# Loading three operands of a gated linear attention kernel with two tokens in a row per partition in place of four

## The chip, the cores and the metric

The kernel runs on one core of a Trainium2 chip. The core has a matrix engine (TensorE, "PE" in the profile), a vector engine (VectorE, "DVE"), a scalar engine (ScalarE, "ACT"), GpSimd ("POOL") and SyncE ("SP"), which in this kernel issues every DMA. Each engine works through its own list of instructions in order and waits on semaphores for the others. The metric is the device time of one execution in microseconds (us); lower is better.

## The reference

The program is a gated linear attention over 768 tokens for 4 batches and 8 heads of 48 channels, followed by a feed-forward block on the 3072 tokens with 384 channels:

```python
for t in range(S):
    state = alpha[:, :, t, :, None] * state + np.einsum('bhd,bhe->bhde', k[:, :, t], v[:, :, t])
    y[:, :, t] = np.einsum('bhd,bhde->bhe', q[:, :, t], state)

x = attn_out.transpose(0, 2, 1, 3).reshape(B * S, H * D)
h = x @ w_in                       # 384 -> 2048
g = h * np.clip(h + 3.0, 0.0, 6.0) / 6.0
out = g @ w_out                    # 2048 -> 384
```

All inputs of the attention are float32.

## The kernel before

The tokens are cut into 24 chunks of 128 (`j` runs from 0 to 23, six to a batch), and chunks go in pairs (`g`) through the feed-forward block. The heads are held in four pairs (`p`, up to `NP` = 4), each pair on 128 partitions: 48 channels of one head, 16 of padding, 48 of the other, 16 of padding.

For a chunk the attention needs alpha, k and q with the channels on the partitions and the tokens along the free dimension. In DRAM a head's data lie token by token, 48 channels each. For chunks 0 to 5 they are loaded as they lie and transposed on TensorE (L282). For chunks 6 to 23 (`FIRST` is 6) this is done with the DVE's transpose of 32x32 blocks, and the DMA that loads the chunk (`load_akq`, L262) puts the data where these blocks need them. That DMA is split into four, one for each group of 32 partitions: heads of one parity and 32 channels (groups 0 and 2), or the last 16 channels (groups 1 and 3; the load begins 32 channels later, and the end of the row is set to 1.0 by the memsets at L257 the first time a buffer is used). Partition `u` of a group holds the four tokens `4u` to `4u + 3` in a row, 4 x 48 channels for each of four head pairs. So one DMA has 32 x 4 pieces of 192 or 160 floats (768 or 640 bytes). There are two buffers for each of alpha, k and q (`quads`, named `aq`, `kq` and `qq` in the profile).

`by_blocks` (L286) then transposes 4 x 4 blocks for each group of partitions in one DVE instruction. A block gives 32 tokens of one place `v` out of four, and they are written to `4u + v`: neighbours in a block lie four floats, 16 bytes, apart.

From these come, on DVE, the products of alpha backwards and forwards (two scans, L309 and L320), k and q scaled by them (L332), on PE the scores (L346), the update of the state (L429) and the output (L455). From chunk 8 on the scaled k goes token by token again without PE: `turn_k` (word `kt`, L391) transposes blocks in place of the raw k, `write_k` (`kw`, four DMAs, L396) writes them to DRAM, and `read_k` (`kr`, four DMAs, L404) reads them back as `kb`, which the state's update reads. v comes in by two DMAs a chunk (`lv`, L272), outputs leave by L728.

The feed-forward block uses sums of weight and activation blocks (L537 to L541, words `y`, `xc`, `o`) so that fewer products are needed: products into the hidden layer at L600 (word `M`), out of it at L703 (word `P`).

The order of all engines' work is one list of words at the end of the function, `run("""...""")`, read by `steps`. `la.9` loads alpha of chunk 9, `ca.9` transposes it, `lk`/`tk` and `lq`/`tq` do the same for k and q; `O.1.1` stores an output block, `y.22` makes a weight sum. Each engine takes its instructions in the order of the list; nothing is reordered. SP has one in-order queue for all DMAs. A DMA that has to wait for its buffer or for its data holds up all those behind it. A part of the list around chunk 9:

```python
M.2.10 cy.6 ck.7 sc.7.0.2 u.7.1.3 n.2.10.14 M.2.11 qa.7.1 ca.9 la.11 y.22 M.2.6.2
h.2.1 q.8 m.7 e.2.0.0 h.2.0 n.2.11.15 qa.6.0 n.2.18.10 qa.8.1 M.2.12 M.2.19
```

Each DMA signals one of eight semaphores, taken in turn, so a DMA is issued only when the eighth one before it has landed.

Of the kernel before, what the change touches and what calls it, by code (L numbers as in the profile page):

```python
# [17 lines left out]
def kernel(  # L18
# [32 lines left out]
    nc = tc.nc  # L51
    B, H, S, D = q.shape
# [35 lines left out]
    for r in range(NR):  # L88
        for name, pad in (("a", 1.0), ("k", 0.0), ("q", 0.0)):
            t = ring[name, r] = rings[:, 3 * r + "akq".index(name)]  # L90
# [3 lines left out]
    for r in range(NV):  # L94
        t = consts.tile([C, 2, H, 64], FP, tag=f"v{r}", name=f"v{r}")
        nc.gpsimd.memset(t, 0.0)
        vs.append(t)
    for r in range(2):
        t = consts.tile([C, 2, H, HB], FP, tag=f"A{r}", name=f"A{r}")
# [6 lines left out]
    for r in range(2):  # L106
        t = consts.tile([C, NP * W + 1], FP, tag=f"ax{r}")
        nc.vector.memset(t, 0.0)
        aX.append(t)
        t = consts.tile([C, NP * W], FP, tag=f"ini{r}")  # L110
# [122 lines left out]

    BLK = 32
    V = C // BLK
    FIRST = 6
    NQ = 2
    quads = {}
    for r in range(NQ):
        for name in "akq":  # L240
            quads[name, r] = consts.tile([C, NP, V, D], FP, tag=f"{name}q{r}",
                                         name=f"{name}q{r}")

    def rows(t, j):
        b, c = divmod(j, NC)
        return t[b, :, c * C : (c + 1) * C, :]

    def load_akq(name, j):
        src = rows({"a": alpha, "k": k, "q": q}[name], j)
        if j < FIRST:  # L250
            nc.sync.dma_start(out=ring[name, j % NR][:, :, 0:D],
                              in_=src.rearrange("h s d -> s h d"))
            return
        to = quads[name, j % NQ]
        if j < FIRST + NQ:
            for o in (BLK, 3 * BLK):
                nc.gpsimd.memset(to[o : o + BLK, :, V - 1, D - BLK : BLK], 1.0)  # L257
        to = to.rearrange("r p v d -> r p (v d)")
        t = src.rearrange("(p a) (u v) d -> a u p (v d)", a=2, v=V)
        for o in range(4):  # L260
            skip = BLK * (o % 2)
            nc.sync.dma_start(out=to[BLK * o : BLK * (o + 1), :, 0 : V * D - skip],  # L262
                              in_=t[o // 2, :, :, skip : V * D])

    v_t = {}

# [7 lines left out]
    def transposed(name, j, i=None):  # L274
        if j >= FIRST:
            t = (K_t if name == "k" else Q_t)[j] = (Ks if name == "k" else Qs)[j % 2]
            by_blocks(t, name, j)
            return
        t = bank("t" + name, j, i)
        src = ring[name, j % NR]  # L280
        for p in range(NP):
            nc.tensor.transpose(  # L282
                t[:, p], src[:, 2 * p : 2 * p + 2].rearrange("s h d -> s (h d)"), ident)

    def by_blocks(to, name, j):
        nc.vector.transpose(out=to.rearrange("r p (u v) -> r p v u", v=V),  # L286
                            in_=quads[name, j % NQ][:, :, :, 0:BLK])

    def reverse(t, first, n):

# [3 lines left out]
    def without_first(t):  # L294
        return t[:, 0 : NP * W].rearrange("r (p w) -> r p w", w=W)[:, :, 1:W]

    def place_alpha(j):
        to = without_first(aX[j % 2])
        if j < FIRST:
            nc.scalar.copy(out=to, in_=ps_t.pop(("ta", j)))  # L300
        else:
            by_blocks(to, "a", j)
# [21 lines left out]
    def scaled(name, j):  # L324

        if j < FIRST:
            src = ps_t.pop(("t" + name, j))
# [244 lines left out]
    for i in range(8):  # L572
        r, o = divmod(i, 3)
# [70 lines left out]
    t = {1: b[0, 1], 2: spare[:, 0], 3: spare[:, 1], 4: spare[:, 2]}  # L644
# [80 lines left out]
    def store2(g, i):  # L725
# [5 lines left out]

    steps = {
        "la": lambda j: load_akq("a", j), "lk": lambda j: load_akq("k", j),
        "lq": lambda j: load_akq("q", j), "lv": load_v, "w": load_weight,
        "d1": round_low, "d2": magnitude, "dx": sign, "d3": high_bits, "d4": add_low,
        "ta": lambda j, *i: transposed("a", j, *i), "tk": lambda j, *i: transposed("k", j, *i),
# [202 lines left out]
```

## Time and profile before

The median of three runs is 539.71 us (539.61 to 539.85). The table is of one profiled execution.

| what | value |
|---|---|
| span of the profiled execution | 538.1 us |
| PE, weight loads, DVE, ACT, POOL busy | 526.3, 499.7, 475.3, 259.6, 50.4 us |
| granted PE clock | 1.00 in all stretches |
| DMA | 54.40 MB in 124101 packets, 101 GB/s on average |
| alpha, k and q loads of chunks 6 on | 216 DMAs, 96 or 80 KB each, about 2.5 us from issue to landing |
| transposes by L286 | 54, 60.2 us in all |

"Busy" counts an engine's own instructions; the issue of a DMA does not count. In groups of instructions the two numbers behind the bar are the total busy time and the mean time of one in nanoseconds; then follows how long the engine stood idle just before them. In lists of waits the numbers are the total, how many, and the longest. In timelines the first number is the start, the second the length, both in us, of a row of equal instructions. "SPq" is the queue of SP.

### The profile page before, as it was taken

The numbers are of one execution on the slowest core, as the hardware profiler recorded it, in microseconds if no ns is written. First come the engines' busy times: TensorE is split into PE (matmuls) and PEld (weight loads), VectorE is DVE, ScalarE is ACT, GpSimd is POOL, SyncE is SP. The second block draws the span as 40 slices with busy tenths as digits, with TensorE's granted clock in tenths as the row PEclk, the third lists the DMA queues.
The fourth block names the chain that finished last, engine by engine and source line by source line (L and its number), as shares of the span: only waits on it lengthen the run. The fifth ranks groups of instructions, "written<-read, shape, count | busy, mean of one in ns | idle before, by whom it ended". The sixth has DMA issues, their size and how long they took to land.

```text
span 538.1 us, 15166 instructions
## 1 busy us (share of the span) xinstructions
PE 526.3 (98%) x6306; PEld 499.7 (93%) x6306; DVE 475.3 (88%) x839; ACT 259.6 (48%) x513; POOL 50.4 (9%) x71
## 2 busy tenths in 40 slices
PE   8799999999999999999999999999999999999997
PEld 7688886789999999999999999999999999999996
DVE  6999989999999899989999898999999898495481
ACT  3889865212653553543544444642644544553230
POOL 5333425100000000000010000000000000000000
PEclk9999999999999999999999999999999999999999
DMA  9998876006625156263444355155354042100001
GB/s 172 211 251 250 218 217 154 17 2 154 149 35 117 30 117 141 46 140 86 94 109 112 89 121 137 21 127 120 88 136 103 15 103 42 44 3 1 15 16 37
DMA packets 124101, 54.40 MB, mean 101 GB/s; under 512 B 83329, under 2 KB 116865, under 8 KB 124033
## 3 DMA queue, kind: packets, MB, share of 16 engines
q1 hardware_dynamic: 124032, 53.44, 43.7%
q8 instruction: 49, 0.80, 0.7%
q14 instruction: 20, 0.16, 0.1%
HBM read 44.50 MB, written 8.91 MB: 99 GB/s over the span
## 4 chain that ended last, share of the span: by engine, by line
PE 83%; DVE 10%; DMA 3%; ACT 1%; issue 1%; SPq 0%; POOL 0%; DVEq 0%; ACTq 0%; POOLq 0%
PE m_ps L703 32%; PE m_ps L600 32%; PE m_ps L478 6%; PE t_ps L455 4%; PE t_ps L346 2%; PE t_ps L429 2%; DMA v<-in_v_dram 2%; PE m_ps L532 1%; PE m_ps L489 1%; PE m_ps L516 1%; DVE rings L647 1%; DVE R L309 1%; DVE raw L537 1%; DVE g_sb L647 1%; DVE w L537 1%
## 5 line engine op out<-in xcount | busy, mean ns | idle before, releaser
L703 PE MATMUL m_ps<-w,g_sb 128*128 128x192 f32 x704 | 122.1, 327 | 0.6 <-ACT m_ps L709 0.5
L606 ACT COPY g_sb<-m_ps 128x512 f32<-128x512 f32 x110 | 63.5, 584 | 114.7 <-PE m_ps L600 98.2
L703 PEld LDWEIGHTS m_ps<-w,g_sb 128*128 128x128 f32 x704 | 113.7, 190 | 1.7 <-ACT m_ps L709 0.8
L703 PE MATMUL m_ps<-rings,g_sb 128*128 128x192 f32 x528 | 91.6, 327 | 0.6 <-ACT u L682 0.6
L703 PEld LDWEIGHTS m_ps<-rings,g_sb 128*128 128x128 f32 x528 | 85.3, 190 | 1.0 <-ACT u L682 0.9
L600 PE MATMUL m_ps<-xc,w 128*128 128x128 f32 x640 | 82.7, 277 | 0.2 <-DVE w L541 0.2
L600 PEld LDWEIGHTS m_ps<-xc,w 128*128 128x128 f32 x640 | 77.5, 192 | 1.4 <-issue 0.4
L494 ACT ACTIVATE r<-g_sb,half 128x512 f32<-128x512 f32 x80 | 56.7, 722 | 29.4 <-DVE g_sb L541 11.7
L498 DVE SCALAR_TENSOR_TENSOR g_sb<-r,g_sb 128x512 f32<-128x512 f32 x80 | 53.6, 682 | 7.5 <-ACT r L494 7.0
L600 PE MATMUL m_ps<-xT,raw 128*128 128x128 f32 x400 | 52.6, 278 | 0.9 <-ACT g_sb L606 0.9
L600 PEld LDWEIGHTS m_ps<-xT,raw 128*128 128x128 f32 x400 | 48.6, 192 | 1.9 <-ACT g_sb L606 1.2
L409 POOL TENSOR_TENSOR st<-sm,R 128x192 f32<-128x192 f32 x20 | 12.9, 643 | 355.8 <-DVE sm L439 306.7
L647 DVE TENSOR_TENSOR g_sb<-g_sb 128x512 f32<-128x512 f32 (+1 forms) x55 | 42.0, 792 | 1.4 <-PE m_ps L703 1.1
L600 PE MATMUL m_ps<-xT,w 128*128 128x128 f32 x320 | 42.0, 276 | 0.0
L600 PEld LDWEIGHTS m_ps<-xT,w 128*128 128x128 f32 x320 | 39.3, 192 | 0.1
L366 ACT COPY A<-q 48x256 f32<-48x256 f32 x88 | 35.6, 404 | 4.9 <-DVE q L332 3.7
L356 DVE TENSOR_TENSOR A<-t_ps,mask 64x256 f32<-64x256 f32 x96 | 36.1, 414 | 0.4
L478 PE MATMUL m_ps<-xT,w 128*128 128x256 f32 x144 | 32.8, 382 | 0.0
L600 PE MATMUL m_ps<-xc,raw 128*128 128x128 f32 x240 | 31.8, 276 | 0.0
L309 DVE TENSOR_TENSOR_SCAN R<-t,ones 128x516 f32<-128x516 f32 x24 | 29.5, 1231 | 1.3 <-ACT t L300 1.2
L478 PEld LDWEIGHTS m_ps<-xT,w 128*128 128x128 f32 x144 | 26.7, 190 | 3.6
L600 PEld LDWEIGHTS m_ps<-xc,raw 128*128 128x128 f32 x240 | 29.6, 192 | 0.1
(105 smaller groups left out, 730.0 us busy)
## 6 DMA issues: line engine op xcount, KB each, us to landing
raw<-in_moe_w_out_dram SPq DMA_DIRECT2D x8, 768.0 KB, 4.8
raw<-in_moe_w_in_dram SPq DMA_DIRECT2D x6, 768.0 KB, 7.0
v<-in_v_dram SPq DMA_DIRECT2D x48, 96.0 KB, 3.2
out_dram<-oh SPq DMA_DIRECT2D x44, 96.0 KB, 1.8
far<-kq SPq DMA_DIRECT2D x64, 64.0 KB, 2.2
kb<-far SPq DMA_DIRECT2D x64, 64.0 KB, 2.0
aq<-in_alpha_dram SPq DMA_DIRECT2D x36, 96.0 KB, 2.6
qq<-in_q_dram SPq DMA_DIRECT2D x36, 96.0 KB, 2.5
```

Source lines behind the costliest of these rows:

```text
L309: nc.vector.tensor_tensor_scan(out=reverse(R, n - 1, n), data0=reverse(ax, n, n), data1=reverse(ones, n, n), initial=0.0, op0=ALU.mult, op ...
L356: nc.vector.tensor_tensor(out=to[:, a], in0=sc[a][half], in1=mask[half, half].unsqueeze(1).to_broadcast([HB, NP, HB]), op=ALU.mult)
L366: nc.scalar.copy(out=to[:, a], in_=Q_t[j][64 * a : 64 * a + D, :, half])
L409: nc.gpsimd.tensor_tensor(out=st, in0=sm, in1=R_t[j][:, :, 0:1].to_broadcast([C, NP, D]), op=ALU.mult)
L455: nc.tensor.matmul(y_of(j, (i + 1) // 2, p)[:, HB * b : HB * b + HB], vb[:, p, e : e + 32], A_t[j][:, b, 2 * p + a], start=(b == 0 and i = ...
L478: nc.tensor.matmul(h[:, f], w1[:, kk, o : o + C], xT_t[g][:, kk], start=(kk == 0), stop=(kk == KT - 1))
L494: nc.scalar.activation(out=to, in_=h, func=AF.Relu, bias=half, scale=1.0 / 6.0)
L498: nc.vector.scalar_tensor_tensor(out=to, in0=r, scalar=1.0, in1=h, op0=ALU.min, op1=ALU.mult)
L600: nc.tensor.matmul(acc[g][i][:, f * C : (f + 1) * C], spots[w][:, f * C : (f + 1) * C], x_of(g, x), start=(first and f == 0), stop=last, s ...
L606: nc.scalar.copy(out=slots[z], in_=acc[g][i])
L647: nc.vector.tensor_tensor(out=out, in0=in0, in1=in1, op=ALU.subtract)
L703: nc.tensor.matmul(to[g], a, rhs[:, f], start=(first and f == 0), stop=(last and f == HF - 1), skip_group_check=True)
```

## The change

A new constant `X` = 2 says how many tokens lie in a row on a partition. The chunk's 128 tokens are cut into two halves (`w`), and in each half partition `u` holds the tokens `2u` and `2u + 1` of that half. A DMA covers one half, since the halves are separate pieces in DRAM: each load has eight DMAs in place of four, of 32 x 4 pieces of 96 or 64 floats (384 or 256 bytes). The buffers keep their size. The transposes write a block's tokens two floats, 8 bytes, apart. The memsets now cover the end of both halves. The list of words is unchanged, and every engine but SP has the same number of instructions. Behind the changed functions the line numbers grow by one to four.

```diff
     V = C // BLK
+    X = 2
     FIRST = 6
@@
         if j < FIRST + NQ:
             for o in (BLK, 3 * BLK):
-                nc.gpsimd.memset(to[o : o + BLK, :, V - 1, D - BLK : BLK], 1.0)
-        to = to.rearrange("r p v d -> r p (v d)")
-        t = src.rearrange("(p a) (u v) d -> a u p (v d)", a=2, v=V)
+                nc.gpsimd.memset(to[o : o + BLK, :, X - 1 : V : X, D - BLK : BLK], 1.0)
+        to = to.rearrange("r p (w x) d -> r p w (x d)", x=X)
+        t = src.rearrange("(p a) (w u x) d -> a w u p (x d)", a=2, u=BLK, x=X)
         for o in range(4):
             skip = BLK * (o % 2)
-            nc.sync.dma_start(out=to[BLK * o : BLK * (o + 1), :, 0 : V * D - skip],
-                              in_=t[o // 2, :, :, skip : V * D])
+            for w in range(V // X):
+                nc.sync.dma_start(out=to[BLK * o : BLK * (o + 1), :, w, 0 : X * D - skip],
+                                  in_=t[o // 2, w, :, :, skip : X * D])
@@
     def by_blocks(to, name, j):
-        nc.vector.transpose(out=to.rearrange("r p (u v) -> r p v u", v=V),
-                            in_=quads[name, j % NQ][:, :, :, 0:BLK])
+        nc.vector.transpose(
+            out=to.rearrange("r p (w u x) -> r p w x u", u=BLK, x=X),
+            in_=quads[name, j % NQ].rearrange("r p (w x) d -> r p w x d", x=X)[
+                :, :, :, :, 0:BLK])
```

## The prediction

> **What bounds the kernel now.** I read the page's busy times and chain first, then the DVE's groups by shape, then the waits and the timeline of SP, whose queue issues every DMA, and last the DVE and PE around the first load that is short of time.
>
> ```profile
> span 538.1 us, 15166 instructions
> ...
> PE 526.3 (98%) x6306; PEld 499.7 (93%) x6306; DVE 475.3 (88%) x839; ACT 259.6 (48%) x513; POOL 50.4 (9%) x71
> ...
> PE 83%; DVE 10%; DMA 3%; ACT 1%; issue 1%; SPq 0%; POOL 0%; DVEq 0%; ACTq 0%; POOLq 0%
> ```
>
> TensorE is the bound. A faster DVE can win only what PE idles for it; the windows from 120 to 460 us leave PE idle for 0.23, 0.16, 0.05, 0.90 and 0.35 us, 1.7 us in all. PE's work itself does not change.
>
> ```profile
> L286 DVE STREAM_TRANSPOSE k<-kq 128x512 f32<-128x512 f32 x18 | 20.1, 1118 | 0.0
> ...
> L391 DVE STREAM_TRANSPOSE kq<-k 128x512 f32<-128x512 f32 x16 | 11.1, 696 | 0.0
> L210 DVE SCALAR_TENSOR_TENSOR raw<-raw,w 128x768 uint32<-128x768 uint32 x11 | 10.6, 960 | 0.6
> ```
>
> The transposes that write 16 bytes apart (L286) take 1118 ns; the same size written without gaps (L391) takes 696. L210 writes 8 bytes apart and takes 960 ns for 768 elements: (960 - 696) / 256 = 1.03 ns an element more, the rate of gapless writing.
>
> SP's waits between 122 and 445 us (total, times, longest):
>
> ```profile
> SPq L728 <- DVE oh L723: 72.2, 6, 27.6
> SPq L396 <- DVE kq L391: 17.3, 3, 9.5
> SPq L404 <- DMA far<-kq: 12.8, 13, 2.4
> ```
>
> All rows of that answer sum to 142 us. 27.6 lie before 122.57, so the queue waits 114 of the 323 us that follow. The row of L404 is its own round trip through DRAM: `kr` waits for `kw` to land, however late both are.
>
> ```profile
> 130.32 1.87 SPq L262 DMA_DIRECT2D qq<-in_q_dram  x4
> 132.24 1.86 SPq L262 DMA_DIRECT2D kq<-in_k_dram  x4
> 134.15 4.97 SPq L262 DMA_DIRECT2D aq<-in_alpha_dram  x8
> 139.71 5.09 SPq L262 DMA_DIRECT2D qq<-in_q_dram  x8
> ```
>
> Four issues take 1.9 us, 0.475 each from start to start (median of the 216), the same for 96 and 80 KB. Eight should take 3.8; the last two rows hold one issue each that took 1.2 to 1.5 us longer. I count 18 such between 122 and 445, 0.96 us over the usual on average, one in 11.6 us of issuing (209 us).
>
> ```profile
> 140.12 1.11 DVE L286 STREAM_TRANSPOSE t<-aq 128x512 f32<-128x512 f32 x1
> 141.05 0.70 DVE L537 TENSOR_TENSOR w<-w 128x512 f32<-128x512 f32 x1
> ```
>
> This is alpha of chunk 9. Its last DMA is issued at 135.57 and lands at 137.71, 2.4 us before use. Right behind it stands `y.22`, whose weight sum PE reads at 143.47.
>
> **The change part by part.** *Transposes.* 54 fall from 1115 ns to between 696 and 1115; I take 700, by L210. That is 54 x 0.42 = 22 us less of DVE, nearly all beside PE. On the path it is worth 0 to 1.7 us (PE's idle above); I take 0.2, the one idle time that DVE ends (L600 waiting for w of L541).
>
> *Fill.* The six pairs of L257 memsets grow from 32x4x16 to 32x8x16, on a POOL that is 9% busy: nothing. If one came late, the first loads of its tile would stand behind it; they have 5 us and more.
>
> *DMA pieces.* Pieces become 384 and 256 bytes, 128 a DMA as before, twice as many DMAs. The nearest rows for small pieces are v's, 192 bytes and 512 a DMA: 3.2 us to landing against 2.6. So landing costs between -0.3 (half the bytes) and +0.6 us; I take 0.
>
> *Issues.* 54 loads take eight issues for four: 216 more on SP. The price of one lies between 0.24 (if it went by bytes) and 0.70 (v, step of two L272); I take 0.475, since the shape 32x4 stays and bytes did not matter between 96 and 80 KB. So each load adds 1.9 us to everything behind it: v, `kw`, `kr`, stores. After 122 us there are 48 loads: 91 us, and 91 / 11.6 = 8 more long issues, 7.5 us. Of 114 us of waits that leaves 15, and 12.8 are the round trips: the queue has no slack left. Where loads bunch, it is late.
>
> I follow it from wherever the queue stands level. "Slack" is the time from landing to first reader; waits that vanish when the queue is late are subtracted.
> - Alpha 9: from 122.57, five loads (q7, k8, q8, k9, a9) add 9.5 us; slack 2.4; 7.1 late on DVE, 6.7 with its own transpose faster. PE's product 6 had 1.7 us in hand after `y.22` (141.75 to 143.47), and the scores of chunk 8 had 1.0 after k.8 (147.42 to 148.44). PE loses 6.7 - 1.0 = 5.7.
> - `kr` 11: from 186.27, five loads, 9.5, minus a wait of 0.5; landing 216.46, update at 221.75, slack 5.3: 3.7.
> - `kr` 13: from 247.04, q14 and q15, 3.8; 258.87 to 261.08 is 2.2: 1.6.
> - v 17: from 268.66, eleven loads, 20.9, minus waits of 2.8, 5.1, 0.8 and 0.4; 11.8 late; 338.10 to 341.63 is 3.5: 8.3.
> - q 19: from 347.54, three loads, 5.7, minus 0.9; slack 2.4; DVE 2.4 late, PE between 0 and 2.4: I take 1.0.
>
> The loads in front of these five come to 49 us of extra issue, 4 long issues; I take 3 us for them, since one may fall on a wait. Before 95 us the first six loads add 11 us beside waits of 1.6 to 6.9 us for POOL; their readers have 5 us and more: nothing, up to 2.
>
> Sum: 5.7 + 3.7 + 1.6 + 8.3 + 1.0 + 3 - 0.2 = 23.1. The profiled execution, 538.1, becomes 561.2. The median of the three runs, 539.71, is 1.6 above its span, so 563.
>
> On the issue price the Trainium skill ("DMA: Bandwidth & Descriptors", section "Issuing engines are not separate DMA queues") says that the time in which a sequencer initiates a DMA is "usually small relative to the DMA itself". For one DMA the rows agree, 0.475 against 2.5 us to landing; for 470 on one in-order queue they do not, and by that rule alone the sum would be -0.2.
>
> **The rivals.**
> - *Issues get cheap (faster).* If an issue's time goes by its bytes, eight cost what four did and only the transposes count: 539.7 minus 0.2 to 1.7, about 538.8. It decides from some 0.30 us an issue: then alpha 9's five loads add 2.5 us, its slack. Against it: 96 and 80 KB cost the same, and `kb<-far` takes 0.46 with 64 KB. For it: no row has exactly these pieces.
> - *The queue catches up.* Once PE has lost 5.7 us, all later releases come later while SP does not, and the waits taken as fixed grow. Then only alpha 9, about half of the rest and no long issues count: 5.7 + 7.3 = 13, or 551 to 553. For it: 114 us of waits. Against it: the loads bunch between waits.
> - *PE slows after its stalls.* At the start PE runs 128x128 matmuls 203 ns apart and later 112 to 150:
>
> ```profile
> 1.46 6.91 PE L532 MATMUL m_ps<-ident 128*128 128x128 f32 x34 [1.46 <-POOL ident masks.py:199]
> ...
> 9.08 0.61 PE L532 MATMUL m_ps<-ident 128*128 128x128 f32 x4
> ```
>
> The slow start lasts about 6 us and costs 2.9. If an idle PE falls back to it, the stalls of 5.7 and 8.3 (perhaps 3.7) cost 2.9 each: 6 to 9 more, 569 to 572. Nothing in this trace shows PE idle that long after its start. The Trainium skill ("TensorE: Matmul & The Clock Gate", "Part 1: The HAM clock gate") gives an idle window of about 3.4 us for the halving; no run here shows it yet.
> - *Transposes stay at 1115.* Hardly any difference here, at most 1 us: PE waits for SP.
>
> **How the numbers follow.** Forecast, stalls worth 18 to 29 us: 0.57. Catching up: 0.20. Slower PE: 0.16. Cheap issues: 0.07, two thirds of it faster by over 0.2% (about what the measurement can tell from no change), the rest within. So faster 0.05, same 0.02, slower 0.93. The predicted time is 563. The range must leave out 2 in 10: 549 takes in most of the catching up, 576 most of the slower PE with an issue step near 0.49; the forecast alone would be 557 to 569.
>
> **What the profile after would show.** The L286 groups (now some lines further down) near 700 ns; DVE busy about 450 us. The load's line on SP with 432 issues, 0.43 each. DVE idle some 6 us ahead of alpha 9's transpose, ended by its DMA; PE idle there and before the updates of chunks 11 and 17, ended by DMAs of kb and v. SP's wait for `oh` far below 72 us. Issues near 0.24 us, or loads that start before the stores which they now stand behind, would make the forecast wrong.

## The result

The changed kernel takes 575.01 us (median; 574.55 to 575.53), the kernel before it in the same comparison 539.78 (539.61 to 540.3): 1.0653 times as long by these medians; the ratio estimated from all executions is 1.0663, with a 95% interval of 1.065 to 1.0675. The forecast was 563, with a range of 549 to 576: the direction was right, the size 12 us too small. One execution of the run with three places mended fell into a slow state of the chip (1086.47 us) and is left out of that run's numbers.

The page of the changed kernel: its span, the busy times, TensorE's granted clock in 40 slices, the DMA queues and the chain that ended last.

```profile
span 573.7 us, 15441 instructions
...
PE 539.3 (94%) x6306; PEld 511.6 (89%) x6306; DVE 458.2 (80%) x839; ACT 260.0 (45%) x513; POOL 50.7 (9%) x71
...
PEclk9899999999799999799999999699998999999999
...
q1 hardware_dynamic: 155136, 51.69, 40.8%
...
PE 72%; SPq 15%; DMA 5%; issue 3%; DVE 2%; POOL 1%; ACT 1%; DVEq 0%; ACTq 0%; POOLq 0%
```

DVE has 17 us less to do (475.3 before) and has left the chain almost wholly (10% before). SP's queue stands in its place: 0% before, 15% now. The row of the clock dips to 7, 7, 6 and 8 around 150, 236, 366 and 437 us, which it did nowhere before. (The 8 in its second slice is half clock from 22.5 to 25.9 us. That lies ahead of the first changed load, at 47 us, and at 36 us PE is 0.5 us ahead of the kernel before.) PE's "busy" time is longer by 13 us although it runs the same 6306 matmuls.

DVE's groups by shape:

```profile
L288 DVE STREAM_TRANSPOSE k<-kq 128x512 f32<-128x512 f32 x18 | 12.7, 704 | 1.5 <-DMA kq<-in_k_dram 1.3 <-DMA kb<-far 0.2
L288 DVE STREAM_TRANSPOSE q<-qq 128x512 f32<-128x512 f32 x18 | 12.6, 702 | 5.0 <-DMA qq<-in_q_dram 5.0
L288 DVE STREAM_TRANSPOSE t<-aq 128x512 f32<-128x512 f32 x18 | 12.6, 702 | 12.3 <-DMA aq<-in_alpha_dram 9.9 <-DMA out_dram<-oh 1.4 <-issue 1.0
```

The transposes fell from 1112 to 1118 ns to 702 to 704. The last column is new: DVE now stands idle ahead of them, 12.3 us ahead of alpha's, 9.9 of it until alpha's own load lands.

SP's timeline around alpha 9:

```profile
133.32 4.82 SPq L264 DMA_DIRECT2D qq<-in_q_dram  x8
138.19 3.75 SPq L264 DMA_DIRECT2D kq<-in_k_dram  x8
141.99 8.72 SPq L264 DMA_DIRECT2D aq<-in_alpha_dram  x16
150.81 8.41 SPq L264 DMA_DIRECT2D qq<-in_q_dram  x16
```

Eight issues take 3.75 us where nothing disturbs them, 0.47 each, as four took 1.86: the price of an issue did not change when its bytes were halved. There is no gap between the rows. Alpha 9 is issued from 142.0 on; before, from 134.2. The ring of eight semaphores is not what holds SP: eight issues take 3.75 us, a load lands in 2.0, and between 122 and 445 us no issue of a load waits for an earlier DMA.

DVE's timeline at the same place, and then PE's waits over the whole run (total, times, longest):

```profile
148.34 0.71 DVE L288 STREAM_TRANSPOSE t<-aq 128x512 f32<-128x512 f32 x1 [7.54 <-DMA aq<-in_alpha_dram]
148.97 0.65 DVE L541 TENSOR_TENSOR w<-w 128x512 f32<-128x512 f32 x1
```

```profile
PE t_ps L433 <- DMA kb<-far: 9.1, 10, 3.4
PE t_ps L433 <- DMA v<-in_v_dram: 7.7, 2, 7.3
PE m_ps L604 <- DVE w L541: 5.4, 1, 5.4
```

DVE stands still for 7.5 us until alpha 9 lands, and PE for 5.4 us, until the weight sum `w` behind it is there at 149.6. The other long waits of PE are for `kb` and `v`, both issued by SP.

PE after its wait ahead of the update of chunk 11, changed kernel:

```profile
234.03 0.90 PE L433 MATMUL t_ps<-v,kb 64*64 64x48 f32 x13 [3.37 <-DMA kb<-far]
...
235.91 5.31 PE L707 MATMUL m_ps<-rings,g_sb 128*128 128x192 f32 x16
```

The same 16 matmuls in the kernel before:

```profile
222.82 2.87 PE L703 MATMUL m_ps<-rings,g_sb 128*128 128x192 f32 x16
```

They take 5.31 us after the wait and 2.87 without one. The granted clock from 234 to 241 us is 0.51.

Since PE runs the same matmuls in the same order, the start of each can be compared in the two traces. The difference changes at these places only, to within 0.1 us (us; "slow clock" is what the following stretch at half clock adds):

| place | forecast | stall | slow clock |
|---|---|---|---|
| before 130 us | -0.2 | -0.88 | |
| alpha 9 | 5.7 | 7.08 | 2.64 |
| update of chunk 11 (`kr` 11) | 3.7 | 3.44 | 3.26 |
| chunk 13 (`kr` 13) | 1.6 | 1.24 | |
| chunks 15 and 16 | | 3.07 | |
| chunk 17 (v 17) | 8.3 | 7.51 | 2.37 |
| chunk 19 (forecast for q 19; it was kb) | 1.0 | 0.84 | |
| L604 at 429, chunk 20 | | 3.81 | 1.65 |
| L707 at 482 | | -0.38 | |
| long issues, anywhere | 3 | in the rows | |
| sum | 23.1 | 25.73 | 9.92 |

25.73 + 9.92 = 35.65, the whole difference of the two spans (35.6). Of the 0.88, 0.42 falls at 128 us, where PE waited for DVE before; 0.46 falls at 34 us, ahead of the first changed load, and is scatter of the start. The 0.38 at 482 us is a wait of the kernel before (0.35 us for ACT at 446 us, behind DVE's transpose of k) that is gone.

### The profile page after: what moved, and what is told of

Its sections match the earlier page's. It is cut to its first block, busy times and chain, and to the rows that moved or that the text cites. A ratio compares the mean times of both kernels' runs of the same rounds, so it can differ in the third digit from the quotient of the medians.

```text
span 573.7 us, 15441 instructions
## 1 busy us (share of the span) xinstructions
PE 539.3 (94%) x6306; PEld 511.6 (89%) x6306; DVE 458.2 (80%) x839; ACT 260.0 (45%) x513; POOL 50.7 (9%) x71
## 3 DMA queue, kind: packets, MB, share of 16 engines
q1 hardware_dynamic: 155136, 51.69, 40.8%
## 4 chain that ended last, share of the span: by engine, by line
PE 72%; SPq 15%; DMA 5%; issue 3%; DVE 2%; POOL 1%; ACT 1%; DVEq 0%; ACTq 0%; POOLq 0%
PE m_ps L707 27%; PE m_ps L604 24%; SPq L264 10%; PE m_ps L482 6%; PE t_ps L459 4%; PE m_ps L520 4%; PE t_ps L433 2%; PE m_ps L493 2%; SPq L408 2%; DMA kb<-far 2%; PE t_ps L350 2%; SPq L400 2%; DMA far<-kq 2%; DMA v<-in_v_dram 1%; PE t_ps L284 1%
## 5 line engine op out<-in xcount | busy, mean ns | idle before, releaser
L707 PE MATMUL m_ps<-w,g_sb 128*128 128x192 f32 x704 | 123.6, 330 | 0.2 <-ACT m_ps L713 0.2
L707 PEld LDWEIGHTS m_ps<-w,g_sb 128*128 128x128 f32 x704 | 115.2, 192 | 1.5 <-DVE g_sb L502 0.5
L707 PE MATMUL m_ps<-rings,g_sb 128*128 128x192 f32 x528 | 94.1, 333 | 0.6 <-ACT u L686 0.6
L604 PE MATMUL m_ps<-xc,w 128*128 128x128 f32 x640 | 85.7, 283 | 6.6 <-DVE w L541 5.4
L707 PEld LDWEIGHTS m_ps<-rings,g_sb 128*128 128x128 f32 x528 | 87.7, 195 | 1.1 <-ACT u L686 0.9
L604 PEld LDWEIGHTS m_ps<-xc,w 128*128 128x128 f32 x640 | 80.0, 197 | 8.1 <-DVE w L541 5.6
L604 PE MATMUL m_ps<-xT,raw 128*128 128x128 f32 x400 | 53.3, 280 | 1.6 <-ACT g_sb L610 0.9
L604 PEld LDWEIGHTS m_ps<-xT,raw 128*128 128x128 f32 x400 | 49.0, 193 | 2.7 <-ACT g_sb L610 1.2
L604 PE MATMUL m_ps<-xT,w 128*128 128x128 f32 x320 | 43.8, 283 | 0.0
L604 PEld LDWEIGHTS m_ps<-xT,w 128*128 128x128 f32 x320 | 41.0, 199 | 0.1
L433 PE MATMUL t_ps<-v,kb 64*64 64x48 f32 x704 | 18.9, 224 | 18.1 <-DMA kb<-far 9.1
L433 PEld LDWEIGHTS t_ps<-v,kb 64*64 64x64 f32 x704 | 15.8, 138 | 21.7 <-issue 13.1
L604 PE MATMUL m_ps<-xc,raw 128*128 128x128 f32 x240 | 32.1, 277 | 0.0
L541 DVE TENSOR_TENSOR g_sb<-g_sb 128x512 f32<-128x512 f32 x40 | 26.9, 682 | 5.5 <-ACT g_sb L610 5.4
```

Of the source, the lines that this page charges most:

```text
L433: nc.tensor.matmul(ps_t["u", j, b][64 * a : 64 * a + 64, p], kb_t[j][half, p, 64 * a : 64 * a + 64], v_t[j][half, b, 2 * p + a, 0:D], star ...
L541: eng.tensor_tensor(out=out, in0=in0, in1=in1, op=ALU.add if s1 > 0 else ALU.subtract)
L604: nc.tensor.matmul(acc[g][i][:, f * C : (f + 1) * C], spots[w][:, f * C : (f + 1) * C], x_of(g, x), start=(first and f == 0), stop=last, s ...
L707: nc.tensor.matmul(to[g], a, rhs[:, f], start=(first and f == 0), stop=(last and f == HF - 1), skip_group_check=True)
```

## The experiments

Two theories stand against each other at first. The one of the prediction: SP's one queue needs 0.47 us an issue, 216 more of them use up its waits, and loads that PE or DVE needs come late. The rival: it is the smaller pieces, or the new layout, that make the loads slow.

### The layout of before, cut into eight DMAs

Each of the four DMAs is cut into two by head pairs. The pieces are the old ones (768 or 640 bytes), and the transposes write 16 bytes apart.

```diff
-            nc.sync.dma_start(out=to[BLK * o : BLK * (o + 1), :, 0 : V * D - skip],
-                              in_=t[o // 2, :, :, skip : V * D])
+            for h in range(2):
+                at = slice(2 * h, 2 * h + 2)
+                nc.sync.dma_start(out=to[BLK * o : BLK * (o + 1), at, 0 : V * D - skip],
+                                  in_=t[o // 2, :, at, skip : V * D])
```

> The kernel before, with each of its four DMAs a load cut into two by head pairs: eight issues a load as in the changed kernel, but pieces of 768 and 640 bytes, four tokens in a row and transposes that write 16 bytes apart. Theory (the issues on SP): as slow as the changed kernel, 573 to 577 us, with PE waiting before the product behind alpha 9 and the updates of chunks 11 and 17. Rival (the smaller pieces): 539 to 541 us.

Measured: 572.9 us (569.75 to 574.07), 1.0613 of before (1.0583 to 1.0643), 0.1 us below the range stated for the theory and 32 above the rival's. Neither the small pieces nor the new stride is needed for the loss.

### Four empty issues behind each load

```diff
+    extra = []
+    unread = consts.tile([BLK, 64], FP, tag="unread", name="unread")
...
+        for o in range(4):
+            n = len(extra) % 64
+            extra.append(n)
+            nc.sync.dma_start(out=unread[:, n : n + 1], in_=src[0, 0:BLK, o : o + 1])
```

> The kernel before with its four DMAs a load and its layout, and behind each load of chunks 6 on four more DMAs of 32 pieces of 4 bytes into columns that nothing reads: 216 more issues as in the change, with 128 bytes each and no load cut in pieces. Theory 'the time that SyncE takes to issue is the cause, whatever the DMA carries': 0.43 to 0.48 us an issue, and nearly the loss of eight old DMAs a load (572.9), less where the last DMA of the late load itself comes 1.9 us sooner: 562 to 574. Rival 'the cut loads, their packets or bytes are the cause': 539 to 542.

Measured: 572.7 us (570.96 to 575.34), 1.0625 (1.0592 to 1.0659). SP's timeline around alpha 9:

```profile
138.55 1.84 SPq L264 DMA_DIRECT2D kq<-in_k_dram  x4
140.44 1.82 SPq L269 DMA_DIRECT2D unread<-in_k_dram  x4
142.31 2.89 SPq L264 DMA_DIRECT2D aq<-in_alpha_dram  x4
145.24 1.82 SPq L269 DMA_DIRECT2D unread<-in_alpha_dram  x4
```

A DMA of 128 bytes holds SP as long as one of 80 or 96 KB: four take 1.82 and 1.84 us. Here nothing is cut and the loads are those of before, yet nearly all of the loss is there, with PE waiting at the same places (5.6 us for `w`, 6.7 for v, 2.8 for kb). That the issue's time on SP is the cause is shown by this run.

### The stride alone

Loads as before, but the transposes write 8 bytes apart. The tokens of a chunk then stand in another order than the reference's.

```diff
-        nc.vector.transpose(out=to.rearrange("r p (u v) -> r p v u", v=V),
-                            in_=quads[name, j % NQ][:, :, :, 0:BLK])
+        nc.vector.transpose(
+            out=to.rearrange("r p (w u x) -> r p w x u", u=BLK, x=2),
+            in_=quads[name, j % NQ].rearrange("r p (w x) d -> r p w x d", x=2)[
+                :, :, :, :, 0:BLK])
```

> The loads of the kernel before (four issues), with transposes that write 8 bytes apart; tokens of a chunk of alpha, k and q from chunk 6 on then stand in another order, so this leaves out the right order of the tokens. Theory: transposes of 0.70 us, worth what PE idled for DVE around 128 us, 0.2 to 0.9 us: 538.8 to 539.6 us. Rival (DVE a co-bound that gives back more of its 22 us): below 538.

Measured: 538.32 us (538.05 to 538.82), 0.9982 (0.9973 to 0.9991). So 22 us less of DVE are worth 0.9 us of 539.22, because PE is the bound: by the trace 0.4 at 128 us, where PE waited for DVE, and 0.4 at 445 us, where it waited for ACT behind DVE's transpose of k. The gain is at the top of the forecast's 0.2 to 0.9; the time is 0.5 us below the range stated with it, which counted from 539.71.

### One, two or three of the three loads

The change for alpha alone (72 more issues), for alpha and q, and for alpha and k (144 each). The edit for the first, which stands in the load and in the transpose; the others have another condition.

```diff
+        X = 2 if name == "a" else V
```

> The change for alpha alone, 72 more issues in place of 216. Theory (a queue that has room and costs only where it is late against a reader): alpha 9 is 1.9 us late with 2.4 us in hand, the read-back of chunk 11 is 3.8 minus 0.5 late with 5.3 in hand, v of chunk 17 has four loads, 7.6, against waits of 9.1: nothing is lost, 539 to 541 us. Rival (every issue costs its share): a third of 35, about 551 us.

Measured, alpha alone: 538.89 us (538.37 to 540.1), 0.9993 (0.9984 to 1.0002).

> The change made for alpha and q, and not for k: 144 more issues in place of 216 (alpha alone, 72 more: 538.9, nothing lost). Theory 'slack first, then a cliff': SyncE waited for 101 us after 122 us beside the round trips; 32 loads there at 4 x 0.475 us more take 61 us, which fits in on the whole, but the loads of alpha 9 and q that stand together at 142 to 160 us come late: 540 to 548. Rival 'each issue costs its share': 539.2 + 35.3 x 144/216 = 562.7, 558 to 565.

Measured, alpha and q: 549.72 us (547.1 to 550.42), 1.0185 (1.0159 to 1.0211).

> The change made for alpha and k, and not for q: again 144 more issues in place of 216. Theory 'slack first, then a cliff': as with alpha and q, 540 to 548; the late items are alpha 9 and the k loads ahead of the round trips kq - far - kb. Rival 'each issue costs its share': 558 to 565. If this and the run with alpha and q lie more than 5 us apart, the place of an issue in the queue counts more than the number of issues.

Measured, alpha and k: 550.41 us (547.63 to 551.01), 1.019 (1.0161 to 1.0218).

72 issues cost nothing, the next 72 cost 10.5 to 11.2 us, the last 72 cost 24 to 25 us of the 34 that they take to issue. That is no fixed price per issue, and the rival's 558 to 565 is refuted; it is slack that is used up and then missing. My 540 to 548 was 2 us too low. Not all of the last 24 to 25 us is lateness: the half clock costs 9.9 us in the changed kernel, and in the profiled executions with 144 more issues 1.5 (alpha and q) and 5.4 (alpha and k). With alpha and q PE waits in three kinds of place (its waits, total, times, longest):

```profile
PE m_ps L606 <- DVE w L543: 2.9, 1, 2.9
PE t_ps L435 <- DMA kb<-far: 2.0, 3, 1.3
...
PE t_ps L435 <- DMA v<-in_v_dram: 1.3, 2, 0.7
```

The wait of 2.9 us at alpha 9 is followed by a stretch at half clock (145.5 to 148.9 us) that adds about 1.5; I had left the clock out. Whether it is q or k that has the other 72 issues makes no difference that these runs can tell.

### Half of the issues from another engine

The second half of the token pairs is issued by GpSimd, and in another kernel by ScalarE. SP issues as many DMAs as before the change.

```diff
-                nc.sync.dma_start(out=to[BLK * o : BLK * (o + 1), :, w, 0 : X * D - skip],
+                (nc.gpsimd if w else nc.sync).dma_start(
+                    out=to[BLK * o : BLK * (o + 1), :, w, 0 : X * D - skip],
```

> The changed kernel, with the four DMAs of the second half of each load issued by GpSimd in place of SP: same pieces, same layout, SP back at four issues a load. Theory (SP's issues): the time of the kernel before less the gain of the transposes, 538.5 to 541 us, if GpSimd's queue keeps up. Rival (small pieces or more transfers as such): 570 us and more.

Measured, GpSimd: 552.23 us (551.5 to 552.89), 1.0238 (1.0224 to 1.0253). Two thirds of the loss go, but neither number fits. GpSimd's timeline:

```profile
134.60 1.00 POOL L413 TENSOR_TENSOR st<-sm,R 128x192 f32<-128x192 f32 x1 [33.27 <-DVE sm L443]
135.55 2.19 POOL L264 DMA_DIRECT2D kq<-in_k_dram  x4
...
142.05 4.33 POOL L264 DMA_DIRECT2D aq<-in_alpha_dram  x8
```

POOL has one step of the state, `st`, and waits 33 us for its input; the loads stand behind it, and GpSimd's half of alpha 9 is issued from 142.05 us on, no sooner than in the changed kernel. An issue takes 0.55 us on POOL. I had looked at how busy the engine is (9%) and not at what its queue waits for. PE loses 2.97, 1.85 and 1.3 us there, between 143 and 152 us. About 5 us more are lost at 463 us in the same way: the second half of a load of q is issued at 458.1, behind an `st` that waits 15.6 us; DVE waits 4.5 us for that load, PE 3.2 for DVE, and the half clock behind it adds 1.6.

> The changed kernel, but of the eight DMAs of a load the four of the second half of the token pairs (w = 1) are issued by ScalarE's queue; SyncE issues as many as before the change. Theory 'the number of SyncE's issues is the cause': SyncE no longer runs late; ScalarE is 45% busy and takes 216 issues of some 0.45 us, 97 us of its 313 us of idle time. A load can be held up by a wait of ScalarE, but those are shorter than GpSimd's 33 us for sm, so it ends below the 552 of GpSimd: 540 to 550, with stalls (if any) that begin at ScalarE. Rival 'eight DMAs a load cost the same wherever they are issued': 570 to 576.

Measured, ScalarE: 611.8 us (609.74 to 613.11), 1.1341 (1.1316 to 1.1367): the slowest of all, and no theory had it. ScalarE's timeline:

```profile
143.42 4.42 ACTq L264 DMA_DIRECT2D aq<-in_alpha_dram  x8
148.21 4.81 ACTq L264 DMA_DIRECT2D qq<-in_q_dram  x8
153.07 0.72 ACT L498 ACTIVATE r<-g_sb,half 128x512 f32<-128x512 f32 x1 [15.16 <-DMA v<-in_v_dram]
```

From 138 to 153 us ScalarE does nothing but issue and wait for room in the load buffers, and its evictions and activations, which PE and DVE need at once, stand behind. 45% busy was an average here; in its order the engine had no room for a block of 16 issues. (The DMA named as the releaser is the last event that the profile shows; the queue ahead of it explains the time.)

### The order of SP's queue

The number of issues is that of the changed kernel; only their order is another. In the first run five stores move behind the load of alpha 9. `so.1` among them now runs after `bo.0` has filled the same buffer, so that one block of 128x384 of the feed-forward block's output is not the reference's; the same holds for the second run.

```diff
-  la.8 O.1.1 O.1.0 ca.8 ... so.1 ... lv.7.0 O.1.2 ... lk.8 O.1.3 lq.8 lk.9 la.9 la.10
+  la.8 ca.8 ... lv.7.0 ... lk.8 lq.8 lk.9 la.9 O.1.1 O.1.0 so.1 O.1.2 O.1.3 la.10
```

> The changed kernel with five stores of output (four of line 732, one of line 531) moved in the written order from among the loads of chunks 7 to 9 to behind the load of alpha 9. Before the move SyncE stands at the first of them until 121.8 us (22.6 us of wait for oh) and only then issues q 7, v 7, k 8, q 8, k 9 and alpha 9. Nothing else moves. Theory 'a load is late by what stands ahead of it in SyncE's queue': alpha 9 lands in time, its 7.05 us of stall and the 2.56 us of half clock behind it go, the other places keep theirs: 575.0 - 9.6 = 565.4, 563 to 568. Rival 'the total of the issues sets the end, the order only moves the lateness': what is gained there is lost at chunk 11 or later, 573 to 576.

Measured: 564.46 us (562.35 to 565.44), 1.0463 (1.0438 to 1.0488). PE's waits (total, times, longest):

```profile
PE t_ps L433 <- DMA kb<-far: 9.0, 10, 3.4
PE t_ps L433 <- DMA v<-in_v_dram: 7.5, 2, 6.9
```

The wait for `w` has gone from the list and the other two are where they were. Instruction by instruction, PE gains 9.7 us on the changed kernel between 139 and 146 us and then less than 1 us more. Nothing is paid back later.

The second run moves the writing and reading of k 11 and 17 and the load of v 17 as well:

```diff
-  xc.4.10 kt.11 O.2.0 O.2.3 lq.11 ... G.3.1.3 lq.12 kw.11
+  xc.4.10 kt.11 kw.11 O.2.0 O.2.3 lq.11 ... G.3.1.3 lq.12
-  O.4.1 la.19 lq.18 kr.17 ... m.16 lv.17.1 sv.17.0
+  O.4.1 kr.17 lv.17.1 la.19 lq.18 ... m.16 sv.17.0
```

> As the run before, and two more moves in SyncE's order: the writing of k 11 to far straight behind its transpose, ahead of the loads of q 11, alpha 13, k 12, alpha 12 and q 12, and the reading of kb 17 and the load of v 17 ahead of the loads of alpha 19 and q 18. As many issues as in the changed kernel. Theory 'a load is late by what stands ahead of it': chunk 11 (3.5 + 3.2 of half clock) and chunk 17 (7.5 + 1.8) go as well: 575.0 - 9.6 - 6.7 - 9.3 = 549.4, 546 to 553; what is left are the small stalls at chunks 13, 15, 16, 19 and 20. Rival 'the total of the issues sets the end': 570 to 576.

Measured: 565.97 us (564.57 to 567.32), 1.0483 (1.0462 to 1.0504), outside both ranges and no better than with the stores alone. The wait for v has gone, but DVE's timeline at chunk 11 shows a new loss:

```profile
215.89 0.71 DVE L288 STREAM_TRANSPOSE q<-qq 128x512 f32<-128x512 f32 x1 [4.64 <-DMA qq<-in_q_dram]
223.43 0.71 DVE L288 STREAM_TRANSPOSE k<-kq 128x512 f32<-128x512 f32 x1 [6.82 <-DMA kq<-in_k_dram]
```

The writing of k 11 stood until 206 us for its transpose, and the loads of q 11, alpha 13 and k 12 behind it came 4 us later than in the changed kernel. PE waited 9.5 us there, and the granted clock was at half from 218.7 to 228.9 us. Around chunk 11 there are five loads and the round trip in 30 us, so it seems that whatever goes first makes the next one late; other orders were not run. So the last run leaves chunk 11 as it is, and keeps `so.1` ahead of `bo.0`:

```diff
-  la.8 O.1.1 O.1.0 ca.8 ... bo.0 lq.7 ... lk.8 O.1.3 lq.8 lk.9 la.9 la.10
+  la.8 lq.7 lk.8 lq.8 lk.9 la.9 O.1.1 O.1.0 ca.8 ... bo.0 ... O.1.3 la.10
-  O.4.1 la.19 lq.18 kr.17 ... m.16 lv.17.1 sv.17.0
+  O.4.1 kr.17 lv.17.1 la.19 lq.18 ... m.16 sv.17.0
```

> The changed kernel with SyncE's order mended at alpha 9 and at chunk 17, and not at chunk 11, where the run with three places showed no room: the loads of q 7, k 8, q 8, k 9 and alpha 9 ahead of the two stores that SyncE waits at until 121.8 us, and the reading of kb 17 and the load of v 17 ahead of the loads of alpha 19 and q 18. As many issues as in the changed kernel, and all of the reference's output. Theory 'a load is late by what stands ahead of it, and it can be mended where SyncE's queue has waits further ahead': alpha 9 (7.05 + 2.56) and chunk 17 (7.5 + 1.8) go, chunk 11 keeps its 3.5 + 3.2: 575.0 - 9.6 - 9.3 = 556.1, 554 to 559. Rival 'at chunk 17 too the move only makes the next load late': the gain of alpha 9 alone, 563 to 567.

Measured: 557.35 us (556.87 to 558.63), 1.0339 (1.0322 to 1.0357). Half of the loss is gone with no issue less. Part of the gain is not where it was expected: chunk 11 stalls for 2.7 us and no longer falls to half clock (3.9 us gained), while a new wait for a block of `A` at 356 us takes back 2.5 and the half clock behind it 1.7. These nearly cancel, so the number was met partly by luck.

### Idle matmuls in the two stalls

Matmuls of the identity, whose results nobody reads, fill the stalls ahead of the updates of chunks 11 and 17.

```diff
+    def warm(i, n):
+        for _ in range(n):
+            nc.tensor.matmul(banks[i][:, 3 * C : 4 * C], ident, ident, start=True, stop=True)
...
-               O.2.1 tq.12 kr.11 u.11.3
+               O.2.1 tq.12 kr.11 zt.3.16 u.11.3
...
-               K.6.2 m.16 lv.17.1 sv.17.0 u.17.1
+               K.6.2 m.16 lv.17.1 sv.17.0 zt.1.34 u.17.1
```

> The changed kernel, with idle matmuls of the identity into columns of the banks that nothing reads: 16 ahead of the update of chunk 11 and 34 ahead of the update of chunk 17, where TensorE stands still for 3.5 and 7.5 us and then runs at half clock (3.2 and 1.84 us lost by it). Theory 'the slow clock is a cost of its own, on top of the stalls': the two losses go, the half clock is missing from the record at 234 and 364 us, and the time is 575.0 - 5.0 = 570, 569 to 571.5. Rival 'SyncE's queue sets the end': what TensorE gains there it waits for at the next late load, and the time stays at 574 to 576, although the half clock has gone from those two places.

Measured: 572.34 us (569.87 to 573.32), 1.0606 (1.058 to 1.0633). PE's timeline of the profiled execution (569.87) at chunk 11:

```profile
228.77 3.74 PE L540 MATMUL t_ps<-ident 128*128 128x128 f32 x32
232.43 0.60 PE L433 MATMUL t_ps<-v,kb 64*64 64x48 f32 x13
...
233.51 2.87 PE L711 MATMUL m_ps<-rings,g_sb 128*128 128x192 f32 x16
```

The stall lasts as long as it did (3.7 us), and the 16 matmuls behind it take 2.87 us again. The half clock is gone at both places, so it follows from PE standing still. Against the 575.01 of the changed kernel the profiled execution gains 5.1 us; the three others, which have no trace, gain 1.7 to 3.1. (The kernel before was 0.6 us faster in this comparison.) Instruction by instruction, the profiled execution gains 3.1 us at chunk 11 and 2.3 at chunk 17, and gives back 1.5 net at chunks 15 and 16, where PE waits for kb and a new stretch at half clock appears at 320 us; the one at 433 us is that of 439 us in the changed kernel, come sooner. The first theory's number was met by the profiled execution alone, the rival's by none. The intervals of the two kernels do not touch, so the clock has a cost of its own; how much of it comes back as waits in the executions without a trace is open.

No kernel here is faster than before by more than 0.2%. Of those with the reference's order of tokens, alpha alone, 538.89, is the nearest, and it can't be told from no change.

## Why the prediction was right, and where it fell short

*What bounds the kernel.* Right. PE was the bound, and the stride alone gave 0.9 us (0.2 forecast, 1.7 at most).

*Transposes, fill, pieces.* Right: 703 ns against 700 assumed, 22 us in all. DVE's busy time fell only to 458 us ("about 450"), as other groups of DVE measure some 5 us more. The loads' DMAs land in 2.0 us, 0.5 sooner than before, and the DMA engines' share fell from 43.7% to 40.8%, of a longer span (235 us of packet time before, 234 now), so pieces of 384 and 256 bytes cost nothing. I had taken 0 between -0.3 and +0.6.

*Issues.* Right, in the term that carries the sum: the median issue is 0.43 us long and 0.47 from start to start. Empty issues and old pieces gave the same loss. The Trainium skill's sentence that the sequencer's time is "usually small relative to the DMA itself" ("DMA: Bandwidth & Descriptors", section "Issuing engines are not separate DMA queues") is true of one DMA here, 0.47 against 2.0 us, and no guide to 432 on one queue. "The queue has no slack left" was nearly so: SP's waits between 122 and 445 us fell from 142 to 65 us; 27.6 and 22.6 of these lie at one store that leaves before 123 us, so 42 us were left where the prediction had 15. The row of that store in the changed kernel, which had 72.2 us before:

```profile
SPq L732 <- DVE oh L727: 33.6, 3, 22.6
```

*The five places.* Right in kind, and in size within 1.4 us each: 20.1 us in all, where the forecast had 20.3 and 3 more for long issues. Two of the marks that I named are there as drawn: DVE idle ahead of alpha 9's transpose (7.5 us for "some 6"), and PE idle ahead of chunks 11 and 17 for kb and v. At chunk 19 the late item was kb, not q.

*First step that failed: the list of places.* I followed the queue only from where it stood level, to five readers, and took the rest as in time. Chunks 15, 16 and 20 and one L604 product lost 6.9 us more, each between 1.3 and 2.5. At the three chunks it is the update that waits for kb, the reader whose slack I had looked up for two chunks only.

*Second step that failed: the clock.* "PE slows after its stalls" was a rival at 0.16, priced at 6 to 9 us; it happened and cost 9.9. What spoke for it was the slow start of the trace, and the Trainium skill's rule ("TensorE: Matmul & The Clock Gate", section "Part 1: The HAM clock gate"). I gave it little since the trace of before had no stall after the start. But the forecast itself put stalls of 5.7 and 8.3 us there, longer than the window of about 3.4 us that the Trainium skill gives there. The traces agree with it on the halving (granted clock 0.50 and 0.51) and on the window's length: in the changed kernel, stretches last 3.4, 6.8 or 10.2 us. They do not agree that a whole idle window is needed (last section).

*How near the number was.* 575 lies 1 us inside the range, whose upper end was set for the slower PE; the band of the forecast alone, 557 to 569, missed it. The mechanism of the sum was right, and the two terms that it lacked, 6.9 and 9.9 us, were in part made up by its 3 us for long issues, which the five places already held.

*The rivals.* "Issues get cheap" is refuted by the issue times; "the queue catches up" by the starts of PE's instructions, which after 130 us never come closer to those of before by more than 0.4 us, and by the moved stores, whose gain of 9.7 us stays to the end. "Transposes stay at 1115" is refuted by the 703 ns.

The sum, worked out anew: 23.1 forecast, + 6.88 for places not listed, + 9.92 for the clock, - 3.19 because the listed places came to 20.11 with their long issues, where 23.3 was forecast, - 1.06 for the greater gain from the transposes (0.6) and the scatter of the start (0.46), gives 35.65.

## What to carry to other kernels

Price a layout by the DMAs it adds to the queue that issues them, with the time per issue from the trace, and compare the total with that queue's own waits; up to that point the issues are free (72 here), behind it they cost more and more of their whole time (24 to 25 of 34 us for the last 72, half clock included), first where loads bunch. Giving them to another engine moves the bill to that engine's in-order queue, so read what that queue waits for and who waits for its work, not how busy it is. And where TensorE will stand still for a few us, allow for a stretch at half clock behind the stall (1.6 to 3.3 us each in the changed kernel).

## What the hardware did that I had not expected

- Half clock needs no long stall. In the run with two places mended, a wait of 2.36 us at 356 us has half clock behind it (359.0 to 362.4, granted clock 0.50), and one of 2.71 us at 221 us has none (1.00 from 223 to 227). In the changed kernel 1.35 us, followed within 1 us by 0.64, was enough at 437 us. The stretches are multiples of 3.4 us. The Trainium skill ("TensorE: Matmul & The Clock Gate", section "Part 1: The HAM clock gate") has the window run freely; but it asks for an idle window of about 3.4 us, and here far less did.
- The traces tell roughly how much. In each of the eleven that have half clock in mid-run, all changes of the clock lie on one grid of 3.413 us. Of the windows of this grid at full clock (from the first change of the clock to 30 us before the end), those in which PE's matmuls leave more than 1.9 us idle are all followed by half clock (26 of 26), those with less than 1.3 us never (0 of 1582), and between the two it is 10 of 21. The wait of 2.36 us lies within one window; that of 2.71 us is cut by the grid into 1.86 and 0.85. So where a stall falls on the grid can decide, and where the grid starts is known only from the trace itself. What decides between 1.3 and 1.9 us is open.

PE's timeline of the run with two places mended, two rows:

```profile
223.28 0.57 PE L433 MATMUL t_ps<-v,kb 64*64 64x48 f32 x13 [2.71 <-DMA kb<-far]
...
358.51 1.92 PE L459 MATMUL t_ps<-A,v 128*32 128x64 f32 x64 [2.36 <-DVE A L360]
```

- The long issues have a companion. Between 120 and 460 us of the changed kernel, 28 of SP's 540 issues take 0.93 us more than usual, and 27 of these overlap a packet of the queue that fetches instructions (31 packets in that time, each taken as 1 us long); of the 512 ordinary ones, 14 do. Before the change it was 18 of 18, and 18 of 368. This is a coincidence in time, not an experiment.
- The transpose writes 8 bytes apart at 703 ns, against 696 without gaps and 1118 at 16 bytes apart: the price rises somewhere between 8 and 16 bytes.
